# Attention and a mixer on one core: how converted weights are stored and loaded, where the first denominators are summed, and where the next batch is transposed

## The chip, the cores and the metric

The kernel runs on one core of a Trainium2 chip. Its time is the device time of one execution in microseconds. Three runs of the kernel before took 1588.48, 1588.49 and 1591.61 us, a median of 1588.49. One more execution was profiled. The program is built at run time into five instruction streams: TensorE (PE in the profile), VectorE (DVE), ScalarE (ACT), GpSimd (POOL) and SyncE (SP). Each stream is worked in its own order, and streams wait for each other through semaphores.

## The reference

```python
# attention: q, k, v are (8, 12, 448, 64) float32
q_n, k_n = rmsnorm(q, g_q), rmsnorm(k, g_k)      # x / sqrt(mean(x*x) + 1e-6) * g over the 64
scores = (1/8) * q_n @ k_n.T                     # 448 x 448 per head
attn = exp(scores - max); attn /= attn.sum(-1) + 1e-9
x = (attn @ v) laid out as (8, 448, 768)
# mixer, weights are float64
u = x + (relu(x.T @ w_tok1) @ w_tok2).T          # w_tok1 448 x 256, w_tok2 256 x 448
out = u + relu(u @ w_ch1) @ w_ch2                # w_ch1 768 x 1536, w_ch2 1536 x 768
```

## The kernel before, in words

**Attention.** A batch has 12 heads, taken as 6 pairs; there are 48 pairs p and two steps g = 2p + h for each (`att_step`, lines 363 to 397). A step computes half of the scores of a pair with the keys on the partitions (`score`, 259), takes the exponentials on ScalarE straight out of PSUM, and multiplies the half computed a step earlier with v (`av`, 317). The denominators are sums over keys, and so over partitions: `chunk_sums` (306) adds four tiles of exponentials, one add on GpSimd and two on VectorE for a pair, and `denominator` (332) multiplies the sum with a block of ones on TensorE, transposes and inverts it on VectorE and scales the output into the tile uT. Norms (`squares`, `roots`, `scale`) and transposes of q and k (`trans_qk`) for later pairs follow in the same list of items.

**Mixer.** For each batch: uT is transposed into x (`trans_x`, 413), two token products (`tok1`, `tok2`), then both channel products. Each channel product is a scheme with seven block products in place of eight (`ch1`, 495; `ch2`, 549), whose weights are sums of blocks of w_ch1 and w_ch2, formed once and kept in DRAM in slots. `PRODUCTS` (445) says which slot goes with which moving operand. The second channel product falls into a part called single (group 3, seven products of one half) and one called double (group 4, seven products of two halves, 14 in all). At last `trans_y` (598) transposes the result back, and ScalarE's queue stores it.

**Weights.** A weight in float64 is loaded as raw words in chunks of 128 x 512 (`weight_load`, 142). Four chunks hold the token weights, 36 the channel weights. `convert_first` (174: lines 181, 182, 184 on VectorE), `convert_second` (187, two operations on ScalarE) and `convert_last` (196: line 209 on VectorE, line 211 on GpSimd) turn it into float32. `combine` (157) forms four more block sums on GpSimd (161 to 164), issues the store of the eight slots on SP (171), and notes in `st["stored"]` how many stages are stored. `weight_items` (215) puts this into items: item i runs `convert_first` of chunk i, `convert_second` of i-1, `convert_last` of i-2, and then asks for the raw chunk i+2. The raw tiles have four buffers, the staged tiles three.

**Units.** A product reads its weights back in units of 384 KB (`unit`, 468), asked for on SP up to five ahead, into five buffers. Units of a group are not asked for before `st["stored"]` covers the whole group.

**Order.** `merge` (27) interleaves lists of items in proportion to their costs, and this sets the order on every engine. The two steps of each pair of batch 0 run first, merged with items 0 to 7 of the weights (line 652). Then, for each batch b, its mixer is merged with the attention of batch b+1 (lines 654 to 664). In batch 0 the transposes, token products and first channel product are merged with weight items 8 to 29, the single products with the rest, and the double products follow without attention. In later batches attention is merged with the whole mixer, the final y transposes included, and the x transposes of a batch are the first items of its mixer. SP issues all loads of q, k, v, raw chunks and units, and the stores of stages, in this one order.

`Start` (667) loads the first two pairs and normalises them before the rest begins. A second arm of the program, for scores that could overflow, is not entered with these inputs.

Of the kernel before, what the change touches and what calls it, by code (L numbers as in the profile page):

```python
# [22 lines left out]
NQ = 8  # L23
# [21 lines left out]
def whole(ctx, tc, shifted, pre, q, k, v, g_q, g_k, moe_w_tok1, moe_w_tok2, moe_w_ch1, moe_w_ch2, out):  # L45
# [10 lines left out]
    P = 128  # L56
# [19 lines left out]
    raw_pool = pool("raw_pool", 4)  # L76
    cv_pool = pool("cv_pool", 3)
    pre.qk_pool = pool("qk_pool", 3)
    pre.st_pool = pool("st_pool", 4)
    v_pool = pool("v_pool", 2)  # L80
# [51 lines left out]
    def stage_list():  # L132

        l = [(moe_w_ch1, mp, 2 * mp + i, t) for mp in range(KF // 2) for i in range(2) for t in range(KC)]
        l += [(moe_w_ch2, 3, 2, t) for t in range(KF)]
        l += [(moe_w_ch2, 4, m, t) for t in range(KF) for m in range(2)]
        return l
# [19 lines left out]
    def combine(j):  # L157

        w, group, m, t = stages[j]
        q = st.pop("stage")  # L160
        nc.gpsimd.tensor_tensor(out=q[:, 4], in0=q[:, 1], in1=q[:, 3], op=ALU.add)
        nc.gpsimd.tensor_tensor(out=q[:, 6], in0=q[:, 1], in1=q[:, 0], op=ALU.subtract)
        nc.gpsimd.tensor_tensor(out=q[:, 5], in0=q[:, 4], in1=q[:, 0], op=ALU.subtract)
        nc.gpsimd.tensor_tensor(out=q[:, 7], in0=q[:, 2], in1=q[:, 5], op=ALU.subtract)
# [7 lines left out]
        st["stored"] = j + 1  # L172
# [22 lines left out]

    def convert_last(i):
        rows, srcs, dst, split = chunks[i]
        n = columns(i)
        if dst is None:
            st["stage"] = stage_pool.tile([P, NQ, P], F32, name="stage")  # L200
            dst = st["stage"][:, 0:4, :].rearrange("p q n -> p (q n)")
        fold = (lambda a: a.rearrange("p (r c) -> p r c", c=split)) if split else (lambda a: a)
        t = st.pop(("raw", i))
        if srcs[0].dtype != I64:
            nc.gpsimd.tensor_copy(out=dst, in_=fold(t[0:rows, 0:n]))
        else:
            lo, hi = (t[0:rows, 0:n, w] for w in range(2))
            e = st.pop(("cv", i))
            nc.vector.scalar_tensor_tensor(  # L209
                out=e, in0=hi, scalar=0x80000000, in1=e, op0=ALU.bitwise_and, op1=ALU.bitwise_or)  # L210
            nc.gpsimd.tensor_tensor(out=dst, in0=fold(lo.bitcast(F32)), in1=fold(e.bitcast(F32)), op=ALU.mult)  # L211
# [104 lines left out]

    def av(p, h):

        if h == 0:
            st["o", p] = ps_O.tile([P, 512], F32, name="o_ps")  # L320
        e, vt, o = st["e", p, h], st["v", p], st["o", p]
        for i in range(HN):
            kc = h * HN + i
            for a in range(2):
                nc.tensor.matmul(  # L325
                    out=o[a * D:(a + 1) * D, 0:S], lhsT=vt[0:R, a, kc * D:(kc + 1) * D],
                    rhs=e[0:R, a, i, :], start=(kc == 0), stop=(kc == NS - 1))
        st.pop(("e", p, h))
# [3 lines left out]
    def denominator(p):  # L332
# [3 lines left out]
        es = st.pop(("es", p))  # L336
        ps = s_tile("d_ps")
        for a in range(2):
            nc.tensor.matmul(  # L339
                out=ps[a * D:(a + 1) * D, 0:S], lhsT=one_c[0:R, :], rhs=es[0:R, a, :],  # L340
                start=True, stop=True)
# [21 lines left out]
    def att_step(g):  # L363
# [22 lines left out]
        if g < NG:  # L386
# [58 lines left out]
    PRODUCTS = ((0, "B11"), (2, "B21"), (5, "T2"), (6, "T3"), (4, "T1"), (7, "B22"), (3, "T4"))  # L445
# [14 lines left out]
    def unit_list(b):  # L460
# [5 lines left out]
        return l + (double + single if b == B - 1 else single + double)  # L466
# [137 lines left out]
    def mlp_items(b):  # L604
        us = lambda n, cols: n * cols * 4 / 2400
        items = []
        for h in range(2):
            items += [(0.5, lambda j=j: trans_x(b, j)) for j in range(h * NC // 2, (h + 1) * NC // 2)]
            items += [(us(NS, HC), lambda j=j, h=h: tok1(b, j, h)) for j in range(NJ)]
# [230 lines left out]
```

## Time and profile before

| | |
|---|---|
| median of three runs | 1588.49 us |
| the profiled execution | 1589.12 us, its span 1587.2 us |
| granted clock of TensorE, mean | 0.953 |
| TensorE busy, idle | 1426.4 us, 160.8 us |
| VectorE, ScalarE, GpSimd busy | 670.1, 492.2, 508.7 us |
| DMA, mean over the span | 137 GB/s |
| first token product of batch 1, of batch 7 | 391.87, 1458.79 us |

A line of the profile such as "m_ps L564" names the tile written and the line of the kernel that issues the instruction. Matmuls of float32 appear as two instructions each. A row of the waits reads: engine and line, what it waited for, total us, times, longest. In the view by stretches each engine's busy time is followed by its number of instructions, then come the granted clock (1 is full speed), the mean busy share of the DMA engines, and GB/s.

### The profile page before, as it was taken

The numbers are of one execution on the slowest core, as the hardware profiler recorded it, in microseconds if no ns is written. First come the engines' busy times: TensorE is split into PE (matmuls) and PEld (weight loads), VectorE is DVE, ScalarE is ACT, GpSimd is POOL, SyncE is SP. The second block draws the span as 40 slices with busy tenths as digits, with TensorE's granted clock in tenths as the row PEclk, the third lists the DMA queues.
The fourth block names the chain that finished last, engine by engine and source line by source line (L and its number), as shares of the span: only waits on it lengthen the run. The fifth ranks groups of instructions, "written<-read, shape, count | busy, mean of one in ns | idle before, by whom it ended". The sixth has DMA issues, their size and how long they took to land.

```text
span 1587.2 us, 18958 instructions
## 1 busy us (share of the span) xinstructions
PE 1426.4 (90%) x6976; PEld 1058.7 (67%) x6976; DVE 670.1 (42%) x1162; ACT 492.2 (31%) x850; POOL 508.7 (32%) x497
## 2 busy tenths in 40 slices
PE   5878655729999999999999999999999999999998
PEld 2334534528577857777578857777578857787898
DVE  6777857541343225433343225333343225322311
ACT  4654433311333233323333232323233232311110
POOL 2357867651233213321233212331233212321221
PEclk9989878859999999999999999999999999999999
DMA  5447785855145524545145523545155533444354
GB/s 122 109 129 225 220 251 156 239 159 172 43 137 158 146 79 110 148 138 158 37 144 157 146 81 106 147 140 161 33 147 150 147 87 98 135 130 120 100 169 137
DMA packets 229258, 217.10 MB, mean 137 GB/s; under 512 B 98116, under 2 KB 185668, under 8 KB 229156
## 3 DMA queue, kind: packets, MB, share of 16 engines
q1 hardware_dynamic: 205634, 204.55, 44.9%
q10 hardware_dynamic: 23522, 11.24, 2.6%
q8 instruction: 58, 0.95, 0.3%
q14 instruction: 44, 0.36, 0.1%
HBM read 185.86 MB, written 29.88 MB: 136 GB/s over the span
## 4 chain that ended last, share of the span: by engine, by line
PE 79%; DVE 8%; DMA 5%; POOL 4%; issue 2%; ACT 1%; SPq 1%; ACTq 0%; DVEq 0%; POOLq 0%
PE m_ps L564 24%; PE m_ps L507 23%; PE s_ps L268 9%; PE o_ps L325 8%; PE m_ps L426 6%; PE m_ps L434 4%; DMA raw<-in_moe_w_ch_dram 2%; PE d_ps L339 2%; PE t_ps L253 2%; POOL stage L211 1%; DVE es L315 1%; PE t_ps L405 1%; DVE ms L739 1%; DVE raw L182 1%; DVE e_t L209 1%
## 5 line engine op out<-in xcount | busy, mean ns | idle before, releaser
L564 PE MATMUL m_ps<-hb,unit 128*128 128x224 f32 x2016 | 404.1, 359 | 46.0 <-DMA unit<-ws 46.0
L564 PEld LDWEIGHTS m_ps<-hb,unit 128*128 128x128 f32 x2016 | 382.4, 193 | 71.9 <-issue 41.2
L274 ACT ACTIVATE e<-s_ps,rs 112x448 f32<-112x448 f32 x384 | 212.3, 634 | 166.6 <-PE s_ps L268 141.5
L507 PE MATMUL m_ps<-tu,unit 128*128 128x224 f32 x1152 | 231.0, 354 | 1.6 <-DMA unit<-ws 1.6
L507 PEld LDWEIGHTS m_ps<-tu,unit 128*128 128x128 f32 x1152 | 215.5, 190 | 11.4 <-issue 5.6
L507 PE MATMUL m_ps<-uT,unit 128*128 128x224 f32 x864 | 181.0, 361 | 30.4 <-DMA unit<-ws 27.8
L507 PEld LDWEIGHTS m_ps<-uT,unit 128*128 128x128 f32 x864 | 163.6, 194 | 51.0 <-issue 29.8
L268 PE MATMUL s_ps<-qkT 64*112 64x448 f32 x768 | 177.4, 576 | 13.3 <-ACT qkT L255 11.7
L325 PE MATMUL o_ps<-e,vt 112*64 112x448 f32 x768 | 167.0, 556 | 3.7 <-DVE uT L357 3.7
L573 POOL TENSOR_TENSOR uT<-uT,r 128x224 f32<-128x224 f32 (+1 forms) x64 | 62.6, 988 | 259.6 <-DVE r L573 155.1
L573 DVE TENSOR_TENSOR uT<-uT,m_ps 128x224 f32<-128x224 f32 (+1 forms) x80 | 38.9, 502 | 233.6 <-PE m_ps L564 168.0
L311 POOL TENSOR_TENSOR es<-e 112x896 f32<-112x896 f32 x48 | 101.3, 2110 | 109.3 <-PE d_ps L339 106.1
L426 PE MATMUL m_ps<-x,w_sb 112*128 112x384 f32 x256 | 106.1, 571 | 23.0 <-ACT x L409 12.0
L268 PEld LDWEIGHTS s_ps<-qkT 64*112 64x112 f32 x768 | 64.1, 178 | 91.0 <-issue 68.1
L325 PEld LDWEIGHTS o_ps<-e,vt 112*64 112x64 f32 x768 | 46.9, 137 | 114.1 <-issue 105.4
L315 DVE TENSOR_TENSOR es<-es,e 112x896 f32<-112x896 f32 x96 | 117.1, 1220 | 6.9 <-POOL es L311 1.3
L351 DVE STREAM_TRANSPOSE dt<-d_ps 128x448 f32<-128x448 f32 x48 | 31.1, 648 | 193.7 <-PE d_ps L339 193.7
L255 ACT ACTIVATE qkT<-t_ps,g_t 128x448 f32<-128x448 f32 x96 | 57.9, 631 | 168.0 <-PE t_ps L253 161.2
L512 DVE TENSOR_TENSOR r<-m_ps,r 128x448 f32<-128x448 f32 x72 | 44.9, 623 | 153.3 <-PE m_ps L507 89.7
L244 POOL TENSOR_TENSOR qk<-qk,rs 112x512 f32<-112x512 f32 x46 | 48.8, 1081 | 178.9 <-DMA out_dram<-y 44.0
L426 PEld LDWEIGHTS m_ps<-x,w_sb 112*128 112x128 f32 x256 | 54.1, 220 | 67.5 <-ACT x L409 23.3
L512 POOL TENSOR_TENSOR hb<-r,r 128x448 f32<-128x448 f32 x24 | 28.5, 1187 | 208.9 <-ACT r L528 208.9
(67 smaller groups left out, 1332.2 us busy)
## 6 DMA issues: line engine op xcount, KB each, us to landing
unit<-ws SPq DMA_DIRECT2D x336, 384.0 KB, 3.1
raw<-in_moe_w_ch_dram SPq DMA_DIRECT2D x72, 256.0 KB, 3.9
ws<-stage SPq DMA_DIRECT2D x36, 512.0 KB, 3.6
vt<-in_v_dram SPq DMA_DIRECT2D x48, 224.0 KB, 2.7
out_dram<-y ACTq DMA_DIRECT2D x48, 224.0 KB, 3.5
qk<-in_q_dram SPq DMA_DIRECT2D x92, 112.0 KB, 3.4
qk<-in_k_dram SPq DMA_DIRECT2D x92, 112.0 KB, 3.3
raw<-in_moe_w_tok_dram SPq DMA_DIRECT2D x4, 448.0 KB, 4.6
```

Source lines behind the costliest of these rows:

```text
L255: nc.scalar.mul(st["qkT", p][:, i, :], ps[:, 0:S], g_t[:, i:i + 1])
L268: nc.tensor.matmul(out=ps[0:R, 0:S], lhsT=qkT[a * D:(a + 1) * D, 1, kc * R:(kc + 1) * R], rhs=qkT[a * D:(a + 1) * D, 0, :], start=True, st ...
L274: nc.scalar.activation(out=e[0:R, a, i, :], in_=pss[a][0:R, 0:S], func=AF.Exp, scale=st["rs", p][0:R, r:r + 1])
L311: nc.gpsimd.tensor_tensor(out=es[0:R], in0=e[0:R, :, 0, :], in1=e[0:R, :, 1, :], op=ALU.add)
L315: nc.vector.tensor_tensor(out=es[0:R], in0=es[0:R], in1=e[0:R, :, i, :], op=ALU.add)
L325: nc.tensor.matmul(out=o[a * D:(a + 1) * D, 0:S], lhsT=vt[0:R, a, kc * D:(kc + 1) * D], rhs=e[0:R, a, i, :], start=(kc == 0), stop=(kc == ...
L426: nc.tensor.matmul(out=ps[:, 0:HC], lhsT=w1_sb[0:R, c, jc * P:(jc + 1) * P], rhs=st["x", h][0:R, c, :], start=(c == 0), stop=(c == NS - 1))
L434: nc.tensor.matmul(out=ps[:, 0:S], lhsT=st["h1", jc][:, cc * P:(cc + 1) * P], rhs=w2_sb[:, jc].rearrange("p c r -> p (c r)"), start=(jc == ...
L507: nc.tensor.matmul(out=ps[:, j * HS:(j + 1) * HS], lhsT=w[:, t, j, :], rhs=m, start=(t == 0), stop=(t == KC - 1))
L512: add = lambda e, o, x, y: e.tensor_tensor(out=o, in0=x, in1=y, op=ALU.add)
L564: nc.tensor.matmul(out=ps[:, j * HS:(j + 1) * HS], lhsT=st["w"](j, t), rhs=hb[:, HB[what], t, :], start=(t == 0), stop=(t == KF - 1))
L573: add = lambda e, o, x, y: e.tensor_tensor(out=o, in0=x, in1=y, op=ALU.add)
```

## The change

- **Weights.** `combine` keeps seven slots: it overwrites the block that no product reads, and does its sums in three operations for four. The store leaves `combine` and is issued by the next item (`store`). `st["stored"]` counts a stage only when the next one's store is issued, except for the last; a unit that is needed at once is asked for in any case. The raw chunk i+2 is asked for at the start of item i, into one of five buffers. The sign bit is put in by `convert_bits` at the start of an item, in place in the raw tile. The double group is stored before the single one.
- **Order.** 14 weight items in place of 8 are merged with the attention of batch 0. In batch 0, items 14 to 37 lie with the transposes, token and first channel products, the rest with the double products. In every batch attention is merged with the mixer up to the double products; the single products come last, without attention, and between them four of the y transposes and all x transposes of the next batch (`last_items`). The other two y transposes lie between the first token products of the next batch.
- **Denominators.** For the six pairs of batch 0, `av` multiplies each tile of exponentials with the ones too (`ones`), summing in a PSUM tile; `chunk_sums` is left out for them.
- **Start.** g_q and g_k are loaded on GpSimd's queue in place of ScalarE's, the scaling of g_q comes after the first `scale`, and three raw chunks are asked for between the q and k of pairs 2 and 3. The small tiles `ms` and `nt` get a pool of their own.

```diff
-NQ = 8
+NQ = 7
-    raw_pool = pool("raw_pool", 4)
-    cv_pool = pool("cv_pool", 3)
+    raw_pool = pool("raw_pool", 5)
+    cv_pool = pool("cv_pool", 2)
...
+        q = st["stage", j]
+        nc.gpsimd.tensor_tensor(out=q[:, 6], in0=q[:, 1], in1=q[:, 0], op=ALU.subtract)
+        nc.gpsimd.tensor_tensor(
+            out=q[:, 4:6], in0=q[:, 1:7:5], in1=q[:, 3:4].to_broadcast([P, 2, P]), op=ALU.add)
+        nc.gpsimd.tensor_tensor(out=q[:, 1], in0=q[:, 2], in1=q[:, 5], op=ALU.subtract)
+
+    def store(j):
...
-        st["stored"] = j + 1
+        st["stored"] = j if j + 1 < len(stages) else j + 1
...
+    def convert_bits(i):
+        if not 0 <= i < len(chunks) or chunks[i][1][0].dtype != I64:
+            return
+        hi, e = st["raw", i][0:chunks[i][0], 0:columns(i), 1], st.pop(("cv", i))
+        nc.vector.scalar_tensor_tensor(
+            out=hi, in0=hi, scalar=0x80000000, in1=e, op0=ALU.bitwise_and, op1=ALU.bitwise_or)
...
         def one(i):
+            if 3 <= i and i + 2 < len(chunks):
+                weight_load(i + 2)
+            convert_bits(i - 2)
             if i < len(chunks):
                 convert_first(i)
             if 0 <= i - 1 < len(chunks):
                 convert_second(i - 1)
-            if i >= 2:
+            if 0 <= i - 2 < len(chunks):
                 convert_last(i - 2)
-            if i + 2 < len(chunks):
-                weight_load(i + 2)
+            if 0 <= i - 3 - len(first):
+                store(i - 3 - len(first))
...
+    def ones(ps, moving, **kw):
+        for a in range(2):
+            nc.tensor.matmul(
+                out=ps[a * D:(a + 1) * D, 0:S], lhsT=one_c[0:R, :], rhs=moving(a), **kw)
...
+            if p < NPAIR:
+                ones(st["d", p], lambda a: e[0:R, a, i, :], start=(kc == 0), stop=(kc == NS - 1))
...
-        if g < NG:
+        if NPAIR <= p < NP:
             items.append((1.0, lambda: chunk_sums(p, h)))
...
-            if st.get("stored", 0) < stage_end[group]:
+            if st.get("stored", 0) < stage_end[group] and i > u:
                 break
...
+    def last_items(b):
+        single = [(us(6, HS), lambda i=i: ch2(b, 1, i, 0)) for i in range(7)]
+        l = turns(b, [0, 1, KC, KC + 1])
+        if b + 1 < B:
+            l += x_items(b + 1, 0) + x_items(b + 1, 1)
+        return [single[0]] + merge(single[1:-1], l) + [single[-1]]
...
-    then = len(first) + stage_end[3] + 2
-    BEFORE = len(first) + 4
+    BEFORE = len(first) + 10
+    then = len(first) + stage_end[4] + 4
...
+        if b == 0:
+            begin = [it for h in range(2) for it in x_items(0, h) + tok1_items(0, h)]
+            early = merge(begin + early, weight_items(BEFORE, then)) + merge(
+                double, weight_items(then, len(chunks) + 3))
+        else:
+            for _, fn in merge(tok1_items(b, 0), left):
+                fn()
+            early = tok1_items(b, 1) + early + double
         lo = (b + AHEAD) * per + 2
         att = att_items(lo, lo + per) if b + AHEAD < B else []
-        for _, fn in merge(att, early) + late if b == 0 else merge(att, early + late):
+        for _, fn in merge(att, early) + last_items(b):
             fn()
+        left = turns(b, [2, KC + 2])
...
-                nc.scalar.dma_start(
+                nc.gpsimd.dma_start(
                     out=self.g_t[a * D:(a + 1) * D, i:i + 1], in_=g.rearrange("(p o) -> p o", o=1))
```

More of the change, by code (lines that the diff above doesn't have):

```diff
@@ L206, in convert_last @@
         else:
[L207 to L211, printed above, removed]
+            lo, hi = (fold(t[0:rows, 0:n, w].bitcast(F32)) for w in range(2))
+            nc.gpsimd.tensor_tensor(out=dst, in0=lo, in1=hi, op=ALU.mult)
         if i >= len(first):
@@ L335, in denominator @@
             st["uT", b] = uT_pool.tile([P, NC, S], F32, name="uT")
[L336 to L341, printed above, removed]
+        if p < NPAIR:
+            ps = st.pop(("d", p))
+        else:
+            es = st.pop(("es", p))
+            ps = s_tile("d_ps")
+            ones(ps, lambda a: es[0:R, a, :], start=True, stop=True)
         nb = S // 32
@@ L645, in whole @@
     pre.load_qk(2, st)
+    for i in range(2, 5):
+        weight_load(i)
     pre.load_qk(3, st)
```

61 lines of the change are left out of this document (28 added, 33 removed).

## The prediction

> **What bounds the kernel now.** I read the header of the page, then engine busy time by stretches, then the waits inside the slow stretch, then the chain of waits there, then TensorE at one border between batches.
>
> ```profile
> span 1587.2 us, 18958 instructions
> ...
> PE 1426.4 (90%) x6976; PEld 1058.7 (67%) x6976; DVE 670.1 (42%) x1162; ACT 492.2 (31%) x850; POOL 508.7 (32%) x497
> ```
>
> TensorE is busy for 90% of the span, so a gain has to come out of its 161 us of idle time. The stretches say where that lies (columns: stretch, length, busy us and instructions by engine, granted clock, DMA share, GB/s):
>
> ```profile
> 0.00:104.70 104.70, 69.78 (x317) 28.38 (x317) 78.03 (x157) 61.27 (x101) 40.68 (x40) 0.93 0.48 120
> ...
> 145.80:277.00 131.20, 82.59 (x400) 60.70 (x400) 96.14 (x139) 49.25 (x84) 96.54 (x111) 0.83 0.74 219
> ```
> ```profile
> 104.70:385.20 280.50, 187.74 (x846) 137.18 (x847) 165.72 (x249) 91.10 (x155) 172.57 (x209) 0.83 0.68 201
> 120.00:160.00 40.00, 36.88 (x154) 20.86 (x155) 31.21 (x44) 18.51 (x33) 31.09 (x40) 1.00 0.79 233
> 1500.00:1550.00 50.00, 50.00 (x266) 50.00 (x265) 10.26 (x17) 6.12 (x11) 13.73 (x12) 1.00 0.58 172
> ```
>
> The mixer of batch 0 with attention of batch 1 (104.7 to 385.2) holds 93 us of the idle time, the first attention stage 35 us. The waits from 105 to 390 name the cause:
>
> ```profile
> PE m_ps L564 <- DMA unit<-ws: 46.0, 2, 28.1
> PE m_ps L507 <- DMA unit<-ws: 29.4, 4, 16.7
> ```
> ```profile
> SPq L171 <- POOL stage L164: 80.4, 31, 6.7
> SPq L154 <- POOL stage L161: 29.9, 10, 4.6
> ```
>
> TensorE waits 75 us for weight units, and units are late because SP, which takes its DMAs in order, waits 110 us and more for GpSimd: 80 us at the store of a chunk just combined, 30 us at the raw load that needs a buffer just multiplied out. The chain shows the loop:
>
> ```profile
> 286.80 0.38 SPq L171
> 287.28 0.55 SPq L154
> 287.87 4.60 DMA raw<-in_moe_w_ch_dram
> ...
> 294.95 1.30 POOL stage L211
> ...
> 298.38 0.38 SPq L171
> ```
>
> Store, load, landing, conversion, combine, store: 11.6 us a turn with two chunks in flight, though GpSimd and VectorE work only part of it.
>
> **Part 1: loads a chunk earlier, stores a chunk later, fifth raw buffer.** Chunk i+2 is now asked for at the start of item i, into the buffer of chunk i-3, multiplied out an item earlier; the store of stage j stands behind the next chunk's combine. SP's 110 us of waits lose their cause. A load's loop becomes three items long instead of two: multiply 1.30, two issues of 0.55, landing 4.6 and conversion come to about 9 us, so it no longer binds above 3 us an item. What binds next is how fast VectorE and GpSimd convert beside their other work. This trace has a stretch that shows it, 120 to 160, before the first group of units was missed. Here are GpSimd's work on the staged tiles in it and in the stretch after, and the work from 104.7 to 350 on the stage tiles (GpSimd) and on the raw tiles (VectorE, ScalarE, GpSimd):
>
> ```profile
> 120.00:160.00 40.00, 22.38 (x32) 1.00 0.79 233
> 145.80:277.00 131.20, 63.41 (x87) 0.83 0.74 219
> ```
> ```profile
> 104.70:350.00 245.30, 123.13 (x170) 0.81 0.70 204
> ```
> ```profile
> 104.70:350.00 245.30, 92.68 (x130) 21.39 (x32) 49.79 (x34) 0.81 0.70 204
> ```
>
> 32 instructions at five a chunk are 6.4 chunks in 40 us: **6.25 us an item** with TensorE at 92%. From 145.8 to 277, with TensorE held up, it is 7.5 us (87/5 = 17.4 chunks in 131.2). I take 6.2, the nearer to a stage without missed units. Its bounds: 7.5, if that stretch was paced by the engines and not by SP; 5.2, if losing waits lets the engines pack closer (VectorE 92.68/32.5 = 2.85 a chunk, GpSimd 123.13/34 = 3.62; with 2.1 and 1.4 an item of other work, worked out under the rivals, that is 5.0 for each).
>
> The Trainium skill, page "SBUF — State Buffer", section "Who interferes with whom", speaks against any packing: a VectorE instruction in a two-port mode, or with two SBUF inputs against a GpSimd read, shares a port pair with GpSimd under an exclusive lock. By that rule taken whole the two engines take turns; by the row 120 to 160, 31.21 + 31.09 = 62.3 us of them ran in 40. Waiting inside a busy time can hide part of this, so the rule is a rival below.
>
> DMA does not bind: 201 GB/s over 280.5 us is 56.4 MB at a share of 0.68, so 296 GB/s at full share. By these sizes
>
> ```profile
> raw<-in_moe_w_ch_dram SPq DMA_DIRECT2D x72, 256.0 KB, 3.9
> ws<-stage SPq DMA_DIRECT2D x36, 512.0 KB, 3.6
> ```
>
> six chunks done earlier take 6.3 MB away and the dropped slot 1.8 MB: 48 MB, 163 us, in a stage that I make 220 us long.
>
> **Part 2: six more chunks under the first attention, its denominators on TensorE.** The stage converts 8 items before 104.7 now and 14 after. Rows of the first 105 us (two of the chain, two of groups):
>
> ```profile
> 65.73 1.92 PE o_ps L325 x8
> 67.65 0.78 PE d_ps L339 x4
> ```
> ```profile
> L315 DVE TENSOR_TENSOR es<-es,e 112x896 f32<-112x896 f32 x14 | 17.8, 1273 | 2.0 <-POOL es L311 1.3
> L311 POOL TENSOR_TENSOR es<-e 112x896 f32<-112x896 f32 x7 | 15.2, 2178 | 6.0 <-PE d_ps L339 5.3 <-ACT sq L736 0.7
> ```
>
> VectorE loses 12 x 1.273 = 15.3 us and gets 6 x 2.85 = 17.1; GpSimd loses 6 x 2.18 = 13.1 and gets 6 x 3.62 = 21.7, on an engine with 64 us free. TensorE gets 16 products a pair, shaped as those of o_ps, for 4: 2 x 1.92 - 0.78 = 3.1 us, 18 us for six pairs, beside 35 us of idle time. I take **0 for this stage**. If TensorE's cover is gone it costs +18; if the shorter way from exponentials to denominators counts (no adds in VectorE's order), half of the 15.3 and the start below, -10.
>
> At the start the four loads of g leave ScalarE's queue, where they stand ahead of its table load:
>
> ```profile
> 4.39 1.12 ACTq L694 DMA_DIRECT2D g_t<-in_g_k_dram  x2
> 5.54 1.28 ACT L736 ACT_TABLE_LOAD   x1 [5.54 <-issue]
> ```
>
> At most 2.3 us come forward. Against it, SP issues three raw chunks ahead of the q and k of pair 3, five issues of 0.55: I set the two off. The sign bit written in place, the smaller pools, three combine operations for four: nothing beyond the 6.2.
>
> **Part 3: the stage after 104.7.** Planner costs: x transposes, both token products and first channel product weigh 69.2, the 14 double products 31.4, so with the items (24 and 5, at 1.0) the first part takes 72% of attention and the second 28%. How much attention is on TensorE's path I take from the page's chain:
>
> ```profile
> PE m_ps L564 24%; PE m_ps L507 23%; PE s_ps L268 9%; PE o_ps L325 8%; PE m_ps L426 6%; PE m_ps L434 4%; DMA raw<-in_moe_w_ch_dram 2%; PE d_ps L339 2%; PE t_ps L253 2%; POOL stage L211 1%; DVE es L315 1%; PE t_ps L405 1%; DVE ms L739 1%; DVE raw L182 1%; DVE e_t L209 1%
> ```
>
> 9 + 8 + 2 + 2 = 21% of 1587.2 over eight batches is 42 us, 45 with what the first stage has off the chain. The second part is TensorE's: 14 products of 2.27 (row below) + 0.28 x 45 = 44.4, five items beside it. The first part has at most 187.7 - 44.4 - 20.3 = 123 us of TensorE's work, so the items pace it: 24 x 6.2 = 149. Units of both channel-2 groups are asked for only when the next store is issued, so one landing each, 3 us twice. Then seven single products with ten transposes and no attention; the last batch shows their pace:
>
> ```profile
> 1569.04 0.44 PE t_ps L405 x4
> 1569.48 2.27 PE m_ps L564 x12
> ```
>
> 7 x 2.27 + 10 x 0.44 = 20.3. Sum: 104.7 + 149 + 44.4 + 6 + 20.3 = **324.4** for the first token product of batch 1, which now starts at
>
> ```profile
> 385.20 0.45 PE t_ps L405 x4
> ...
> 391.87 5.49 PE m_ps L426 x8
> ```
>
> so 67.5 us are gained.
>
> **Part 4: borders between batches.** One of them, TensorE, VectorE and the granted clock:
>
> ```profile
> 558.77 4.81 PE L564 MATMUL m_ps<-hb,unit 128*128 128x224 f32 x24
> ...
> 571.24 4.51 PE L426 MATMUL m_ps<-x,w_sb 112*128 112x384 f32 x8 [1.56 <-DVE x L411]
> ...
> 579.78 2.85 PE L426 MATMUL m_ps<-x,w_sb 112*128 112x384 f32 x8
> ...
> 584.62 5.43 PE L426 MATMUL m_ps<-x,w_sb 112*128 112x384 f32 x16 [0.68 <-ACT x L409]
> ```
> ```profile
> 564.22 2.28 DVE L315 TENSOR_TENSOR es<-es,e 112x896 f32<-112x896 f32 x2
> ...
> 569.81 1.28 DVE L411 COPY x<-t_ps 112x512 f32<-112x512 f32 x2
> ```
> ```profile
> 572.00:574.00 2.00, 2.00 (x5) 1.09 (x4) 0.00 (x0) 0.00 (x0) 0.07 (x1) 0.50 0.11 30
> ```
>
> The copies of x stand behind VectorE's adds and norms. From 563.6 to 571.24 TensorE has nine transposes of 0.45 to do in 7.7 us: 3.6 lost. The next group runs at half clock: 4.51 - 2.85 = 1.7. Then 0.7 at 584. **6.0 a border**, six of them 35.7, and 5.49 - 2.85 = 2.6 behind border 0: 38. Afterwards the transposes lie between single products, which the rows at 1569 show to run without a gap. What remains open is whether attention, which no longer has the closing 20 us and the first token products of a batch to lie beside, leaves new holes: bounds 20, if each border keeps half of its loss, and 41, if every small wait goes too.
>
> **Sum.** 1587.2 - 67.5 - 38.3 = 1481.4 of span; the profiled execution took 1589.12, 1.9 more than its span, and 0.6 over the median 1588.49. Forecast **1483**.
>
> **Rivals.**
> - Conversion stays at 7.5 an item: + 31, 1514. For it, VectorE and GpSimd are 73% busy there; against it, SP's 110 us.
> - It packs to 5.2: - 24, 1459. For it, per-engine sums; against it, longer operations whenever both run.
> - The first stage follows TensorE: + 18, 1501.
> - The borders give nothing, because closing stretches without attention lose what they gain: + 38, 1521. Rows at 1569 speak against it.
> - VectorE and GpSimd in turns: from 104.7 to 385.2 they do 165.7 - 92.7 = 73 and 172.6 - 123.1 = 49 us beside these tiles' work; 0.7 of it over 24 items is 2.1 and 1.4, and 2.1 + 1.4 + 2.85 + 3.62 = 10.0 an item: 24 x 3.8 more, 1574. It is what the port rule gives; the row at 120 speaks against it.
> - Slower: units come late in the closing stretches. There TensorE uses a unit every 2.27 to 3.2 us, and nothing hides a miss. If each of seven products waits one landing of 3.1 in each of seven stretches: + 152, 1635. It turns the sign from 15 us a stretch, 2.1 a product. For it: every long wait of TensorE now is for units. Against it: 1500 to 1550, where only unit-fed products run, is 50.00 of 50.00 busy.
>
> **Chances.** Forecast 0.43; 7.5 an item 0.20; 5.2 an item 0.17; first stage 0.05; borders 0.06; turns 0.03; late units 0.06. The range 1448 to 1522 takes in the first five, with the first stage's -10 under 1459. A measurement of this kernel tells about 0.2% from no change. Faster by more than that is all but late units, where 0.05 is slower and 0.01 no change: 0.94, 0.01, 0.05.
>
> **What would show it.** SP's waits for GpSimd at the stores and raw loads in batch 0 should fall below 20 us; TensorE's waits for units to two of about 3 us; first token product of batch 1 near 324; chunks 6.2 us apart after 105; from then on a batch every 173 us, for 179 now; at the borders no granted clock of 0.50. A later start of batch 1 with GpSimd or VectorE near 90% busy would mean 7.5; waits for units in the single products, the slower case.

## The result and the profile after

The changed kernel takes **1491.61 us** (median of four runs, 1490.15 to 1492.98) for 1588.49 before: a ratio of 0.9388, 95% interval 0.9371 to 0.9406. The forecast was 1483. Its profiled execution took 1491.37 us with a span of 1489.4, 8.0 over the 1481.4 of the sum. Lines moved with the edit: the conversion on VectorE is now L189, L190 and L192 (before L181, L182 and L184), the sign bit is still L209, the multiply on GpSimd L224 (L211), x is copied at L438 or L436 (L411, L409), the first token product is L453 (L426), and products from units are L534 and L591 (L507, L564).

Busy time by stretches, cut at the first token product of batch 0, ahead of the double products, and at the first token products of batches 1 and 2:

```profile
core 0: us, PE busy (x) PEld busy (x) DVE busy (x) ACT busy (x) POOL busy (x), PEclk, DMA share, GB/s
0.00:118.60 118.60, 78.85 (x388) 33.21 (x388) 85.87 (x169) 67.92 (x113) 48.46 (x60) 0.93 0.67 174
118.60:272.40 153.80, 117.46 (x508) 76.88 (x509) 133.81 (x176) 66.11 (x114) 114.61 (x118) 0.88 0.70 211
272.40:340.90 68.50, 67.47 (x371) 58.62 (x370) 33.39 (x53) 20.12 (x34) 31.52 (x34) 1.00 0.70 210
340.90:512.60 171.70, 171.70 (x873) 129.40 (x873) 66.86 (x122) 54.82 (x96) 44.76 (x38) 1.00 0.45 129
```

From 272 on TensorE has next to no idle time. In the second row VectorE is 87% busy (133.81 of 153.80) and GpSimd 75%: these two set the pace of the conversions, rather than SP, as the run with the old order of stores and loads bears out below: its 24 items take the same time. What TensorE still waits for, from 118 to 390 (total us, times, longest):

```profile
PE d_ps L336 <- ACT e L290: 24.0, 3, 9.4
PE m_ps L453 <- DVE x L438: 17.5, 2, 10.0
...
PE m_ps L591 <- DMA unit<-ws: 1.0, 1, 1.0
```

The waits for units (46.0 us at channel 2 in the rows of before) are down to one of 1.0. The 24.0 us for exponentials go back to the conversions as well: all three waits are for work that stands in ScalarE's queue behind an operation waiting for GpSimd (6.81 us ahead of 229.68, 6.43 ahead of 267.10) or for VectorE (8.80 ahead of 194.33). One of them:

```profile
229.68 0.58 ACT L540 ACTIVATE hb<-hb 128x448 f32<-128x448 f32 x1 [6.81 <-POOL hb L539]
231.99 1.76 PE L336 MATMUL d_ps<-es,one_c 112*64 112x448 f32 x4 [6.07 <-ACT e L290]
```

SP still waits for GpSimd, from 118 to 340:

```profile
SPq L157 <- POOL stage L224: 51.7, 16, 7.8
SPq L179 <- POOL stage L166: 40.6, 27, 6.7
```

So 92.3 us of SP's waits at raw loads and stores remain. They just no longer hold up a unit. TensorE's own steps, from its timeline:

```profile
108.01 0.65 PE L432 MATMUL t_ps<-ident,uT 128*112 128x128 f32 x4 [2.38 <-ACT qkT L271]
118.66 4.89 PE L453 MATMUL m_ps<-x,w_sb 112*128 112x384 f32 x8 [10.00 <-DVE x L438]
...
274.42 1.30 PE L591 MATMUL m_ps<-hb,unit 128*128 128x224 f32 x6
276.74 5.94 PE L591 MATMUL m_ps<-hb,unit 128*128 128x224 f32 x30 [1.03 <-DMA unit<-ws]
...
320.44 2.45 PE L591 MATMUL m_ps<-hb,unit 128*128 128x224 f32 x12
...
340.73 2.75 PE L453 MATMUL m_ps<-x,w_sb 112*128 112x384 f32 x8
```

The prediction had 104.7 for the first of these products and 324.4 for the last; they are at 118.66 and 340.73. The 10 us ahead of 118.66 are a wait for a copy on VectorE, whose timeline there is:

```profile
106.19 0.68 DVE L209 SCALAR_TENSOR_TENSOR raw<-raw,e_t 128x512 uint32<-128x512 uint32 x1
106.91 0.56 DVE L189 TENSOR_SCALAR e_t<-raw 128x512 uint32<-128x512 uint32 x1
107.57 2.38 DVE L190 SCALAR_TENSOR_TENSOR raw<-raw,e_t 128x512 f32<-128x512 uint32 x1
109.99 1.15 DVE L192 TENSOR_SCALAR e_t<-raw 128x512 uint32<-128x512 uint32 x1
111.05 2.87 DVE L331 TENSOR_TENSOR es<-es,e 112x896 f32<-112x896 f32 x2
...
113.84 1.22 DVE L782 TENSOR_REDUCE ms<-sq 112x16 f32<-112x1040 f32 x1
...
117.23 1.28 DVE L438 COPY x<-t_ps 112x512 f32<-112x512 f32 x2
```

A conversion, the first chunk sums and a chain of norms all stand ahead of two copies of 0.6 us each that TensorE waits for.

### The profile page after: what moved, and what is told of

Read it like the earlier page. It is cut to its first block, busy times and chain, and to the rows that moved or that the text cites. A ratio compares the mean times of both kernels' runs of the same rounds, so it can differ in the third digit from the quotient of the medians.

```text
span 1489.4 us, 19019 instructions
## 1 busy us (share of the span) xinstructions
PE 1405.4 (94%) x7048; PEld 1050.6 (71%) x7048; DVE 675.2 (45%) x1150; ACT 488.5 (33%) x850; POOL 485.3 (33%) x459
## 4 chain that ended last, share of the span: by engine, by line
PE 85%; DVE 6%; POOL 3%; issue 2%; ACT 1%; DMA 1%; SPq 1%; ACTq 0%; POOLq 0%; DVEq 0%
PE m_ps L591 26%; PE m_ps L534 23%; PE s_ps L284 9%; PE o_ps L349 9%; PE m_ps L453 6%; PE m_ps L461 5%; PE t_ps L432 3%; PE d_ps L336 2%; PE t_ps L269 2%; DVE raw L190 2%; DVE raw L209 1%; PE m_ps L336 1%; POOL stage L224 1%; DVE e_t L189 1%; SPq L765 1%
## 5 line engine op out<-in xcount | busy, mean ns | idle before, releaser
L591 PE MATMUL m_ps<-hb,unit 128*128 128x224 f32 x2016 | 400.2, 354 | 1.0 <-DMA unit<-ws 1.0
L591 PEld LDWEIGHTS m_ps<-hb,unit 128*128 128x128 f32 x2016 | 374.1, 190 | 20.4 <-issue 14.8
L534 PEld LDWEIGHTS m_ps<-tu,unit 128*128 128x128 f32 x1152 | 217.7, 192 | 20.8 <-issue 17.6
L534 PE MATMUL m_ps<-tu,unit 128*128 128x224 f32 x1152 | 232.0, 357 | 0.0
L284 PE MATMUL s_ps<-qkT 64*112 64x448 f32 x768 | 172.9, 570 | 13.2 <-ACT qkT L271 13.2
L534 PE MATMUL m_ps<-uT,unit 128*128 128x224 f32 x864 | 175.7, 357 | 2.6 <-DVE uT L466 2.1
L534 PEld LDWEIGHTS m_ps<-uT,unit 128*128 128x128 f32 x864 | 162.1, 192 | 15.2 <-issue 11.3
L327 POOL TENSOR_TENSOR es<-e 112x896 f32<-112x896 f32 x42 | 88.8, 2115 | 194.9 <-PE d_ps L336 188.4
L600 POOL TENSOR_TENSOR uT<-uT,r 128x448 f32<-128x448 f32 (+1 forms) x64 | 62.6, 988 | 207.1 <-DVE r L600 166.4
L600 DVE TENSOR_TENSOR uT<-uT,m_ps 128x448 f32<-128x448 f32 (+1 forms) x80 | 38.9, 503 | 172.0 <-PE m_ps L591 167.6
L453 PE MATMUL m_ps<-x,w_sb 112*128 112x384 f32 x256 | 92.8, 508 | 17.5 <-DVE x L438 17.5
L331 DVE TENSOR_TENSOR es<-es,e 112x896 f32<-112x896 f32 x84 | 101.6, 1210 | 12.2 <-ACT e L290 7.9
L453 PEld LDWEIGHTS m_ps<-x,w_sb 112*128 112x128 f32 x256 | 48.7, 198 | 51.4 <-issue 27.2
L461 PE MATMUL m_ps<-w_sb,h 128*128 128x448 f32 x192 | 75.7, 543 | 0.0
```

The source lines that it names most:

```text
L284: nc.tensor.matmul(out=ps[0:R, 0:S], lhsT=qkT[a * D:(a + 1) * D, 1, kc * R:(kc + 1) * R], rhs=qkT[a * D:(a + 1) * D, 0, :], start=True, st ...
L327: nc.gpsimd.tensor_tensor(out=es[0:R], in0=e[0:R, :, 0, :], in1=e[0:R, :, 1, :], op=ALU.add)
L331: nc.vector.tensor_tensor(out=es[0:R], in0=es[0:R], in1=e[0:R, :, i, :], op=ALU.add)
L453: nc.tensor.matmul(out=ps[:, 0:HC], lhsT=w1_sb[0:R, c, jc * P:(jc + 1) * P], rhs=st["x", h][0:R, c, :], start=(c == 0), stop=(c == NS - 1))
L461: nc.tensor.matmul(out=ps[:, 0:S], lhsT=st["h1", jc][:, cc * P:(cc + 1) * P], rhs=w2_sb[:, jc].rearrange("p c r -> p (c r)"), start=(jc == ...
L534: nc.tensor.matmul(out=ps[:, j * HS:(j + 1) * HS], lhsT=w[:, t, j, :], rhs=m, start=(t == 0), stop=(t == KC - 1))
```

## Experiments

Twelve kernels ran, each an edit of the changed kernel. Places below are starts of the first token product of batches 0 and 1 (118.66 and 340.73 unedited). They come from one profiled execution of each kernel; border_before and x_back, which leave the first stage as it is, start batch 0 at 117.79 and 119.46, so a difference of 1 us in these two columns shows nothing.

| kernel | median us | ratio to before, 95% | batch 0 | batch 1 |
|---|---|---|---|---|
| changed | 1491.61 | 0.9371 to 0.9406 | 118.66 | 340.73 |
| eight_items | 1508.64 | 0.9480 to 0.9512 | 117.15 | 359.56 |
| added_sums | 1504.23 | 0.9455 to 0.9486 | 131.85 | 354.22 |
| first_as_before | 1505.84 | 0.9461 to 0.9497 | 113.48 | 355.81 |
| first_before_x_act | 1492.52 | 0.9383 to 0.9414 | 103.25 | 342.20 |
| x_act | 1482.93 | 0.9324 to 0.9355 | 110.54 | 332.52 |
| store_at_once | 1496.85 | 0.9399 to 0.9436 | 120.96 | 349.00 |
| single_first | 1496.95 | 0.9415 to 0.9446 | 119.03 | 345.39 |
| bits_last | 1484.39 | 0.9329 to 0.9361 | 114.08 | 332.84 |
| buffers_only | 1488.49 | 0.9359 to 0.9390 | 116.51 | 336.83 |
| border_before | 1520.12 | 0.9559 to 0.9591 | 117.79 | 341.45 |
| x_back | 1517.24 | 0.9538 to 0.9572 | 119.46 | 341.44 |
| bits_x_act | **1475.88** | 0.9280 to 0.9311 | 105.60 | 324.89 |

### The first stage: its two additions, one at a time

```diff
-    BEFORE = len(first) + 10        # eight_items
+    BEFORE = len(first) + 4
```

> The changed kernel with 8 weight items, not 14, beside the attention of batch 0; the other six go to the stage behind it. Theory (conversions stand in the loop TensorE - VectorE - ScalarE - TensorE of each pair): the first token product starts near 105 in place of 118.7, since each item puts some 3 us of VectorE and 1.4 of ScalarE into the loop; the stage behind has 30 items to run at 6.4, 38 us more; in all about 24 us slower than the changed kernel, near 1516. Rival (the ones products on TensorE lengthen the first stage): the start stays at 118 and the total goes to about 1530.

```diff
-            if p < NPAIR:               # added_sums: no product with ones per tile
-                ones(st["d", p], lambda a: e[0:R, a, i, :], ...)
...
-        if NPAIR <= p < NP:             # chunk_sums for every pair again
+        if p < NP:
```

> The changed kernel with the first denominators summed by GpSimd and VectorE as before, and one product with the ones. Theory of the loop: VectorE gets 15 us back, and since it sets the stage the first token product starts later, 125 to 132, total near 1502. Rival (TensorE's 18 us of ones set the stage): start near 105 to 108, total near 1480.

added_sums does what its theory said: without the products with ones the first token product comes 13.2 us later, and 12.6 arrive at the end. With 14 items in the stage it is VectorE that sets it, and the chunk sums are what it can't take: VectorE is busy for 109.11 of the 131.85 us, GpSimd, which does a third of these sums, for 67.81. eight_items fits neither theory: the start hardly moves (117.15, as the rival had it, for 105 or near it by the loop of conversions), and the total of 1508.64 lies below both. TensorE at the start of these two, eight_items first, with its first double product:

```profile
117.15 5.24 PE L453 MATMUL m_ps<-x,w_sb 112*128 112x384 f32 x8 [12.41 <-DVE x L438]
...
292.86 6.38 PE L591 MATMUL m_ps<-hb,unit 128*128 128x224 f32 x24 [3.02 <-DMA unit<-ws]
```
```profile
131.85 3.54 PE L446 MATMUL m_ps<-x,w_sb 112*128 112x384 f32 x5 [10.01 <-DVE x L431]
```

Six items fewer, and still 12.41 us of waiting for the copy of x. That made the copy the next suspect.

The rows also say why the total came out low. From the first token product to the first double product 30 items take 292.86 - 117.15 = 175.7 us, where 24 take 155.8 in the changed kernel. Six more items cost 20.0 us there (3.02 of them a wait for a unit), 3.3 an item, and not the 38 of the expectation; between x_act and first_before_x_act below it is 16.6. So 6.4 us an item is no price of an item: by an estimate from these figures, about half of it is time that the stage takes whatever the number of items.

### The first stage: both additions undone, and the copy of x

first_as_before has both edits above; x_act has only this one, and first_before_x_act has all three:

```diff
-        turn(b, j, st["x", half][0:R, :, o:o + P], j % 2)
+        turn(b, j, st["x", half][0:R, :, o:o + P], j % 2 or b == 0)
```

> The changed kernel with both additions to the first attention undone: eight weight items beside it as before instead of fourteen, and denominators from sums over the tiles instead of a product with ones per tile. Stores, slots and borders stay as changed. This is the first stage for which the prediction took 104.7 us. Theory (the two additions alone made the first stage 14 us longer, one through VectorE, the other through TensorE): first token product at 103 to 108, then 30 items at 6.4, batch 1 at 344 to 350 (340.89 in the changed kernel), 1494 to 1501 us. Rival (the reordered loads, stores and slots slow the first stage by themselves): first token product at 112 or later, total 1503 or more.

> The changed kernel with all copies of x of batch 0 on ScalarE; the changed one gives every other of them to VectorE, where they stand behind conversions, sums and norms (TensorE waits 10.0 us for one ahead of 118.66 and 7.5 ahead of 139.20, while ScalarE is idle for 11). Theory (VectorE's queue, not its load, makes the first token product late): it starts at 106 to 112 instead of 118.66, the wait of 17.5 us for VectorE at the first token products goes, and some 5 to 12 us of it arrive at the end: 1480 to 1487 us. Rival (VectorE's load in the conversions is the limit, 87% busy from 118 to 272, so an earlier start only waits later): double products begin within 3 us of 276.7, 1488 to 1493.

> The changed kernel with eight items beside the first attention and its denominators from sums, and all copies of x of batch 0 on ScalarE. With the first two alone TensorE waited 12.2 us for VectorE's second copy of x, between which and the first a whole conversion lies (107.22 and 112.65), and the first token product came at 113.48. Theory (the place of that copy is what the changed order of batch 0 cost the first stage beside the two additions): first token product at 101 to 106, as before the change, and 1494 to 1499 us. Rival (VectorE is simply later, by the longer conversions, and the copy only shows it): 109 or later, or batch 1 within 3 us of 355.8, 1503 to 1507.

The theory of first_as_before fell, and its rival held: with both additions gone the first token product comes at 113.48, not near 105. VectorE and TensorE of first_as_before there:

```profile
107.22 0.68 DVE L431 COPY x<-t_ps 112x512 f32<-112x512 f32 x1
107.82 0.68 DVE L209 SCALAR_TENSOR_TENSOR raw<-raw,e_t 128x512 uint32<-128x512 uint32 x1
108.54 2.15 DVE L189 TENSOR_SCALAR e_t<-raw 128x512 uint32<-128x512 uint32 x1
110.72 1.41 DVE L190 SCALAR_TENSOR_TENSOR raw<-raw,e_t 128x512 f32<-128x512 uint32 x1
112.17 0.56 DVE L192 TENSOR_SCALAR e_t<-raw 128x512 uint32<-128x512 uint32 x1
112.65 0.68 DVE L431 COPY x<-t_ps 112x512 f32<-112x512 f32 x1
113.48 0.98 PE L446 MATMUL m_ps<-x,w_sb 112*128 112x384 f32 x1 [12.25 <-DVE x L431]
```

The merge of batch 0 has other lists than before, and it put a whole conversion between the two copies. The other two runs tell whether that place, or VectorE's load, is what counts. TensorE's start in x_act, then in first_before_x_act:

```profile
110.54 5.12 PE L453 MATMUL m_ps<-x,w_sb 112*128 112x384 f32 x8 [0.87 <-ACT x L436]
```
```profile
103.25 4.48 PE L446 MATMUL m_ps<-x,w_sb 112*128 112x384 f32 x8 [2.48 <-ACT x L429]
```

Copies on ScalarE start batch 0 8.1 us earlier, all of it is kept to batch 1 (8.2), and 8.7 arrive at the end. With the additions undone too, the start is 103.25, as before the change (104.69). The theories held; for first_before_x_act the time fell 1.5 us under the range given. So of the 14.0 us by which the changed kernel is late at this point, 8.1 are the copies' place and 110.54 - 103.25 = 7.3 the two additions; the rest, -1.4, is hardly more than these places vary.

The last two rows also give what the additions are worth where no copy is in the way: 1492.52 - 1482.93 = 9.6 us. In the changed kernel as it stands, undoing one cost 17.0 or 12.6, and undoing both 14.2: they can't be summed.

### The order of stores and raw loads

```diff
-    raw_pool = pool("raw_pool", 5)
+    raw_pool = pool("raw_pool", 4)
-        st["stored"] = j if j + 1 < len(stages) else j + 1
+        st["stored"] = j + 1
...                 # in an item: the store right behind combine, then the raw load
```

> The changed kernel with loads and stores as before: four raw buffers, the load at the end of an item, the store right behind the combine. Theory (SP's order paced the conversions): items go from 6.4 to 7.0 to 7.5 us, the first token product of batch 1 comes 15 to 25 us later, total 1507 to 1517. Rival (VectorE and GpSimd pace them in any case): within 5 us of 1491.

The theory fell, and the rival was right to within 1 us: 1496.85, 5.2 us over the changed kernel, for 15 to 25. Waits for units do come back, but small (TensorE, 118 to 390):

```profile
PE m_ps L534 <- DMA unit<-ws: 5.0, 1, 5.0
PE m_ps L591 <- DMA unit<-ws: 4.0, 2, 2.2
```

Batch 1 starts 8.3 us later than in the changed kernel, in the profiled execution, which at 1499.53 us was the longest of the four. None of it is the pace of the items: from the first token product to the first double product, at 276.61, it takes 155.7 us, as in the changed kernel. 2.3 us come from the first stage and 6.1 from behind the first double product.

### The order of the two channel-2 groups in batch 0

```diff
-        return l + double + single
+        return l + (single + double if b == 0 else double + single)
...                 # stages, and items beside the single products, to match
```

> The changed kernel with batch 0's channel-2 order as before: the chunks and units of the seven single products come first and their products lie beside the last items, the fourteen double products close the batch beside y turns and x transposes. So 18 items lie beside the first part, for 24, and 11 beside seven products of 2.27 us, for 5 beside fourteen. Theory (the order of the two groups is a large part of the gain in batch 0: with the short group in the middle the last conversions have too little of TensorE's work beside them): first part 18 x 6.4 = 115 from 118.66, then 11 x 5 to 6.4 = 55 to 70, then 14 x 2.27 and ten transposes of 0.44 = 36 and two landings: batch 1 at 331 to 346 if the items pace it all the way, plus what the units cost because their chunks are stored last; I take 10 to 30 us back in all: 1502 to 1522 us, with waits for units in the double products of batch 0. Rival (all conversions have to be done before the closing stretch either way, and the order only decides which products wait): within 6 us, 1486 to 1498.

The rival held: 1496.95, 5.3 over. A wait of 7.9 us for a unit shows. But the merge also shifted in this kernel, and TensorE waits for VectorE's copies of x for 2.5 us instead of 17.5:

```profile
PE m_ps L591 <- DMA unit<-ws: 7.9, 1, 7.9
...
PE m_ps L453 <- DVE x L438: 2.5, 1, 2.5
```

So 5.3 us is a net figure. The order of the groups by itself can be worth more, by an estimate from these two waits up to 15 us more.

### VectorE's conversion and GpSimd's multiply

One mean in the list of groups stands out, that of L190, here in the changed kernel, with its counterpart of before behind it:

```profile
L190 DVE SCALAR_TENSOR_TENSOR raw<-raw,e_t 128x512 f32<-128x512 uint32 x36 | 52.8, 1466 | 2.8
```
```profile
L182 DVE SCALAR_TENSOR_TENSOR raw<-raw,e_t 128x512 f32<-128x512 uint32 x36 | 33.5, 931 | 1.2
```

The same operation takes 1466 ns for 931. VectorE and GpSimd in the changed kernel, early on:

```profile
23.33 0.70 DVE L190 SCALAR_TENSOR_TENSOR raw<-raw,e_t 112x512 f32<-112x512 uint32 x1
...
34.06 1.26 POOL L224 TENSOR_TENSOR w_sb<-raw 112x512 f32<-112x512 f32 x1 [3.34 <-DVE raw L209]
34.47 1.34 DVE L190 SCALAR_TENSOR_TENSOR raw<-raw,e_t 128x448 f32<-128x448 uint32 x1
```

Where GpSimd is idle it takes 0.70 us; where GpSimd's multiply began 0.41 earlier it takes 1.34, and ends 0.49 after the multiply. In the new order that is the rule: the sign bit (L209) releases the multiply, and L189 and L190 come right behind. By the timeline, 39 of the 40 executions of L190 begin while a GpSimd operation runs, 26 of them while L224 does, and each ends 0.48 to 0.63 us after that operation; the one that begins alone is the one of 0.70. The Trainium skill, page "SBUF — State Buffer", section "Who interferes with whom", has VectorE operations with two SBUF inputs and GpSimd share a port pair under an exclusive lock, and the ends of these 39 agree with it.

```diff
-    cv_pool = pool("cv_pool", 2)                   # both
+    cv_pool = pool("cv_pool", 3)
-    stage_pool = pool("stage_pool", 3)             # both, to make room
+    stage_pool = pool("stage_pool", 2)
-            convert_bits(i - 2)                    # bits_last only
             if i < len(chunks):
                 convert_first(i)
+            convert_bits(i - 2)
```

> The changed kernel with the sign bit put in behind the three VectorE steps of the newer chunk (three buffers for the exponents, two for the staged tiles in exchange). Theory (GpSimd's multiply, which starts as soon as the sign bits are in, lies on top of VectorE's second step and stops it): that step falls from 1.47 to about 0.93 us as in the kernel before, VectorE loses 0.5 us an item, and with VectorE 87% busy in the stage behind 118.6 the total falls by 8 to 15 us, to 1477 to 1484. Rival (the two engines only change who waits): the step gets shorter, GpSimd's multiply longer, and the total stays within 4 us of 1491.

> The changed kernel with three e_t buffers for two and two stage buffers for three, the sign bits where they were: the pools of the kernel with the sign bits last, without its order. Theory (the order on VectorE gave that kernel its 7.2 us, through shorter conversions): 1489 to 1496 us, and the conversion at L190 stays at 1.4 to 1.5 us. Rival (the third e_t buffer gave it): 1482 to 1486.

L190 in bits_last, then in buffers_only:

```profile
L190 DVE SCALAR_TENSOR_TENSOR raw<-raw,e_t 128x512 f32<-128x512 uint32 x36 | 39.4, 1096 | 2.8
```
```profile
L190 DVE SCALAR_TENSOR_TENSOR raw<-raw,e_t 128x512 f32<-128x512 uint32 x36 | 50.3, 1398 | 2.8
```

With the sign bit behind the conversion, 26 of the 40 executions still begin while GpSimd is busy (27 before the change), and the others take 0.63 to 0.70 us. L190 falls to 1096 ns, not to the 0.93 us of its theory, and the kernel gains 7.2 us, just short of the 8 to 15. The pools alone give 3.1 of these and leave L190 at 1398, so neither account of buffers_only was whole: about 4.1 us belong to the order.

### The borders

```diff
-        if b + 1 < B:                              # both: no x transposes in the closing part
-            l += x_items(b + 1, 0) + x_items(b + 1, 1)
...
+            for _, fn in x_items(b, 0) + merge(tok1_items(b, 0), left):      # x_back
+            early = x_items(b, 1) + tok1_items(b, 1) + early + double
...
+            early = [... x_items(b, h) + tok1_items(b, h)] + early + double  # border_before
+        for _, fn in merge(att, early + last_items(b)):     # border_before, from batch 1 on
+        return [single[0]] + merge(single[1:-1], l) + [single[-1]] + turns(b, [2, KC + 2])  # border_before
```

> The changed kernel with the borders between batches as they were: the transposes of x and the first token products open a batch, attention is merged through the closing products too from batch 1 on, and the four y turns follow the last product. The conversions and the first stage stay as changed. Theory (the 46.8 us gained after batch 1's first token product are all the border's): a batch every 179 us again and 46.8 back, 1536 to 1541 us; granted clock of 0.50 behind the first token products again. Rival (the stretches between the borders gained too, since the changed first token products and the order of attention beside them pack closer): 20 to 36 back, 1512 to 1528.

> The changed kernel with one thing undone at the borders: the transposes of x for the next batch go back to that batch's start, ahead of its first token products; the closing products keep the y turns and stay without attention, and the two late y turns stay beside the first token products. Theory (the loss at a border is TensorE waiting for the last copy of x, and the low clock that follows it): 4 to 7 us a border come back, 24 to 42 in six, 1516 to 1534 us, and the first token products of a batch wait for VectorE or ScalarE at x. Rival (it was attention beside the closing products that cost, through the late adds and norms ahead of the copies): with VectorE free there the copies follow their transposes at once, at most 2 us a border, 1492 to 1504.

In border_before two y transposes, not four as its text says, follow the last product, since the group that closes a batch is still the short one. A border of the changed kernel (TensorE), then of border_before (TensorE and VectorE), then of x_back:

```profile
510.13 2.44 PE L591 MATMUL m_ps<-hb,unit 128*128 128x224 f32 x12
512.41 2.75 PE L453 MATMUL m_ps<-x,w_sb 112*128 112x384 f32 x8
```
```profile
514.21 0.65 PE L432 MATMUL t_ps<-ident,uT 128*112 128x128 f32 x4 [0.35 <-ACT qkT L271]
...
515.30 1.28 DVE L438 COPY x<-t_ps 112x512 f32<-112x512 f32 x2
516.73 3.99 PE L453 MATMUL m_ps<-x,w_sb 112*128 112x384 f32 x8 [1.87 <-DVE x L438]
```
```profile
517.36 2.82 PE L453 MATMUL m_ps<-x,w_sb 112*128 112x384 f32 x8 [0.87 <-DVE x L438]
...
526.03 2.85 PE L453 MATMUL m_ps<-x,w_sb 112*128 112x384 f32 x8 [1.09 <-ACT x L436]
```

A batch, averaged over the five from batch 1 to batch 6, takes 179.13 us before, 171.67 after, 176.25 in border_before and 175.91 in x_back. The place of the x transposes is therefore worth 4.2 us of the 7.5 a batch, and what border_before undoes beside it (attention beside the closing products, the two late y turns) next to nothing more (0.3). By their totals the rival held for border_before (28.5 back) and the theory for x_back (25.6). But the clock in x_back is 1.00, without the low clock of its theory, and VectorE has no adds or norms to do ahead of its copies. TensorE is busy for 172.6 of the 175.9 us there: of 3.3 idle, 0.87 and 1.09 are the waits for copies of x above and 1.3 are for exponentials. So transposes directly ahead of the products that need them cost this even where VectorE has nothing else to do.

The remaining 2.9 us a batch neither run undid, but the rows of TensorE show where it lies. Its token products over six batches, before the change and in border_before:

```profile
L426 PE MATMUL m_ps<-x,w_sb 112*128 112x384 f32 x208 | 86.7, 574 | 17.5 <-ACT x L409 9.7 <-DVE x L411 7.8
```
```profile
L453 PE MATMUL m_ps<-x,w_sb 112*128 112x384 f32 x192 | 70.6, 519 | 14.4 <-DVE x L438 9.3 <-ACT x L436 5.1
```

With 32 of them a batch, 574 ns for 519 are 1.8 us. In the same stretches TensorE waits 8.1 us ahead of transposes of x and y before the change and 1.9 in border_before, over six borders: 1.0 a border. Both runs still close a batch with the short group, so that two y transposes and not four are left after the last product; that this is the cause is an argument, not a measurement.

### Both gains together

> The changed kernel with the sign bits behind the next chunk's first conversions (three e_t buffers, two stage buffers) and all copies of x of batch 0 on ScalarE. Alone these gave 1484.4 and 1482.9 us for 1491.6. Theory (they work at different places: the collision of VectorE's conversion with GpSimd's multiply paces the items, the copies set the start): the gains add, 1474 to 1478 us, batch 1 at 323 to 327. Rival (both shorten the same queue of VectorE at the same place): 1480 to 1484.

This is bits_last with the copies of x of batch 0 on ScalarE. The gains add, as the theory had it: 7.2 + 8.7 = 15.9 were to be had, and 15.7 came. At **1475.88 us** it is 0.9295 of the kernel before (0.9280 to 0.9311) and the fastest of all. TensorE:

```profile
105.60 2.85 PE L453 MATMUL m_ps<-x,w_sb 112*128 112x384 f32 x8 [1.33 <-ACT x L436]
...
324.89 2.75 PE L453 MATMUL m_ps<-x,w_sb 112*128 112x384 f32 x8
```

## Why the prediction was right, and where not

The changed kernel is 6.1% faster, and both of its parts are the ones that the prediction named: batch 0, where units no longer make TensorE wait (51.1 us gained for 67.5 forecast), and the borders (46.7 from there to the end for 38.3). The sum came within 8.0 us of the span, but by errors of both signs, so that its closeness is in part luck:

| term | predicted | measured | difference |
|---|---|---|---|
| first token product of batch 0 | 104.7 | 118.66 | +14.0 |
| from there to the first double product (items, a landing) | 149 + 3 | 155.8 | +3.8 |
| double products | 44.4 | 46.0 | +1.6 |
| closing single products (and a landing) | 20.3 + 3 | 20.3 | -3.0 |
| from batch 1's first token product to the end | 1157.0 | 1148.7 | -8.3 |

- **Part 2, "I take 0 for this stage"**, is the term that was mis-sized. The additions cost 7.3 us there, within the bounds of -10 and +18 but not at 0. The other 8.1 are a step that the prediction left out: it followed which operations VectorE gains and loses, but not behind which of them the copies of x come to stand once the lists are merged anew. It had quoted just this at a border (copies "behind VectorE's adds and norms") and did not ask it of batch 0. The rival with the first stage at +18 (1501) had the size nearly right, through TensorE; the 10.00 us wait ahead of 118.66 is for VectorE. The total did not go there, since the borders gave more.
- **Part 1, 6.2 us an item**, held as a rate for this stage: 155.8 / 24 = 6.5. The rivals at 7.5, 5.2 and 10.0 an item are out. Its reason held only in part. SP's waits for GpSimd did not fall below 20 us, they are 92.3; and with stores and loads back in the old order the 24 items take 155.7 us all the same, and the kernel loses 5.2 us, not the 31 between 6.2 and 7.5 an item. VectorE at 87% and GpSimd at 75% set the pace. Nor do items alone make up the stage, as 24 x 6.2 has it: 30 of them take 175.7 us (eight_items), and in that stretch VectorE is busy for 156.63 us in place of 135.66, 3.5 more for each item. The rest of its 135.66, about 50 us by this estimate, is other work. So taking six items out of this stage was worth 20 us and not 6 x 6.2 = 37.
- **Turns of VectorE and GpSimd**: as a rate for the whole stage it fell, yet single operations show the lock (39 of 40 executions of L190), and moving one operation away from it gave about 4 us. The prediction had weighed it for the stage only; its remark that waiting inside a busy time can hide part is what L190 shows.
- **Part 3**, one landing for each channel-2 group, 3 us twice: one of 1.03 us was seen, none ahead of the single products. Their seven products with ten transposes took 340.73 - 320.44 = 20.3, as worked out.
- **Part 4, 6.0 us a border**, was too little: 7.5. The mis-sized term is the low clock. Over the same five batches TensorE is busy for 175.3 of 179.1 us a batch before and for all of the 171.7 after. The 3.8 of idle time that went are near the 4.3 worked out (3.6 and 0.7); the 3.6 of busy time are twice the 1.7 put down for the clock, and 2.7 of them are the 32 token products at 574 ns before and 489 after. The granted clock of such a batch was 0.98 or 0.99 before; it is 1.00 through the last stretch above. How much of this the adds and norms ahead of the copies caused is not shown: x_back gives back 4.2 us without them and at full clock. Nothing was lost by attention having less to lie beside: TensorE is busy 171.70 of 171.70.
- **The slower case**, units late in the closing stretches, did not come about; no such wait is in those stretches.

**Open.** Batch 1 starts 51.1 us earlier than before (391.87 to 340.73). Undone from the changed kernel, the first stage gives back 15.1 of them, the order of stores and loads 8.3, the order of the groups 4.7. Some 23 are in none of these alone. The groups and the stores were not undone together, and the seven slots, the three combine operations and the sign bit in place were not undone at all. The combine operations took GpSimd as long as before, 80.2 us for the three and 81.2 for the four.

## What to carry to other kernels

When lists of work are merged into one order for each engine, find the short operations that the bound engine waits for, and look at what the new merge puts ahead of them: here two copies of 0.6 us behind 11 us of other work on VectorE cost the kernel 8.7. Put such an operation on the engine that is idle at that moment, and put an operation that releases a neighbour behind the one which that neighbour would disturb. Do not take a stage's time divided by its items for the price of one more item; here it was 6.5 us against 3.3. Undo the parts of a change singly and together before their gains are summed; here 17.0 and 12.6 were 14.2 together.

## What was not expected of the hardware

A VectorE operation with two SBUF inputs went from 0.70 to 1.34 us when a GpSimd multiply of 1.26 us had begun just ahead of it, and to 2.38 (at 107.57) behind a GpSimd add of 2.25 that began at 107.15. In 39 of 40 cases it ended about half a microsecond after the GpSimd operation that it had begun under. The order of two lines moved its mean over 36 executions from 1398 to 1096 ns with the same buffers.
